# Two transfers of the first batch, a weight slice and a query load, issued later in a hand-ordered attention and gated-MLP kernel on one Trainium2 core

## The chip, the cores and the metric

One core of one Trainium2 chip runs the whole kernel in one launch. The metric is the device time of one execution in microseconds (us), the median over runs. The engines are named as in the profile: PE (matmul), ACT (activations), DVE (VectorE), POOL (GpSimd) and SP (SyncE, which here only issues transfers). Each engine works through its own instructions strictly in order; an instruction that waits holds all that stand behind it.

## The reference

Four batches of eight heads, 768 positions, 64 values per head. Each query and key gets a bucket number from the signs of six random projections; a query attends only to the keys in its bucket. The 3072 x 512 result goes through a gated MLP with a residual.

```python
q_bits = (np.einsum('bhsd,dk->bhsk', q, proj) > 0).astype(np.int64)
k_bits = (np.einsum('bhsd,dk->bhsk', k, proj) > 0).astype(np.int64)
mask = q_bucket[:, :, :, None] == k_bucket[:, :, None, :]
scores = np.where(mask, scale * np.matmul(q, k.transpose(0, 1, 3, 2)), -1000000000.0)
attn = softmax(scores)                  # written out in the reference
x = np.matmul(attn, v)                  # heads side by side: 3072 x 512
gelu = 0.5 * g * (1.0 + erf(g * inv_sqrt2))          # g = x @ w_gate
ffn_out = gelu * (x @ w_val) @ w_out
out = x + 1.0 / (1.0 + np.exp(-(x @ w_res))) * ffn_out
```

## The kernel before

The heads are worked on in pairs: pair p holds two heads, four pairs make a batch, and there are 16 pairs. A pair has nine *chunks* of scores (1024 columns of PSUM each); chunk c belongs to pair c // 9, so that the first batch is chunks 0 to 35 and its fourth pair, p = 3, is chunks 27 to 35. One chunk is some score matmuls (`scores`, L501), one exponential on ACT (L512), and the matmuls with the values (`values`, L476), which the plan places a chunk or more later.

The mask needs no extra pass. The six signs of each query and key are appended to their 64 values as columns of +0.5 and -0.5, one more column holds a constant, and the score matmul contracts over 71 rows, so that a key in another bucket comes out far below. The steps that bring a side of a pair there are, for side 0 (queries) and 1 (keys):

- `load` (L161): the raw values from HBM into `ld`, on SP's queue, 384 KB. `load_v` (L169) does it for the values.
- `tr` (L273) on DVE and `hash` (L284) on PE: the projections, on which the signs depend; `tokens` (L296) brings them back on DVE.
- `cast` (L263 for queries, L265 for keys): the values in bf16 into one of four tiles `nat`.
- `bits` (L305): the signs into `nat`, in four parts of 32 partitions, each on the engine that a letter names: `'vvvp'` is three on DVE and one on POOL.
- then `nat` is transposed into `aug`, either on PE (`turn`, L374, with copies out of PSUM at L382) or by a DMA transpose on SP's queue (`turn_dma`, L361). In the first batch only pair 3 goes by DMA: `('turn_dma', 3, 0)` and `('turn_dma', 3, 1)`.

`vals_a` and `vals_s` (plan names `va` and `vs`, L387 and L395 to L399, on POOL) prepare the values of a pair. `finish` (L420, L421) divides by the sums into `x_tok`; for the first two pairs of the first batch a DMA transpose on SP (L429) follows, from `x_tok` into `x_sb`, for the others PE transposes (`xturn`).

The MLP's weights are bf16 tiles, read from fp32 in HBM by transfers that POOL issues (`load_w`, L248, plan name `w`). There are twelve in a fixed order: first slices of 384 columns, alternately of `w_gate` (`wg`) and `w_val` (`wv`), four each, then `wr`, then three of `wo`. Each `w` in the plan issues the next one. The plan of the first batch has two, so the second is the first slice of `wv`; the other ten are spread over the first gate stage by another list, `BESIDE_GV`. The gate stage (`gv_mm`, L526) follows the 36 chunks; its `wv` matmuls are the first readers of the second transfer.

The order of the first batch is written out by hand, as the list `PLAN` (L17 to L76): it is worked through from first to last, each entry calls the function of its name in `STEP` (L707), and the instructions stand on each engine's queue in the order in which these calls make them. `('S', c)` is the scores and the exponential of chunk c, `('V', c)` its values. Waits between engines follow from the tiles that they share. SP's queue in this stretch is: the loads of the first pairs, the key load of pair 6, the transpose of `x_sb`, the query load of pair 6, the two transposes of pair 3, and then loads of pairs 5 to 7 with a second `x_sb` transpose among them. `ld` has four tiles a side, so a load waits until the pair four back is through.

From the second batch on, a loop with lists of due places takes the part of the plan.

Of the kernel before, what the change touches and what calls it, by code (L numbers as in the profile page):

```python
# [44 lines left out]
    ('S', 12), ('hash', (2, 3), 2), ('hash', (2, 3), 3), ('copy', 1, 1, 6, 12, 'v'), ('cast', 2, 1, 'p'),  # L45
    ('cast', 2, 0, 'p'), ('hash', (2, 3), 0), ('hash', (2, 3), 1), ('finish', 0, 0), ('tokens', (2, 3)),
    ('bits', 2, 0, 'vvp'), ('bits', 2, 1, 'vp'),
# [6 lines left out]
    ('S', 19), ('bits', 3, 0, 'vvvp'), ('turn_dma', 3, 0), ('vs', 2), ('turn', 2, 1, 6, 12, 'f'),  # L54
# [740 lines left out]
```

## Time and profile before

| | |
|---|---|
| time, median of 3 runs | 341.25 us (341.06 to 341.38) |
| the profiled execution: its time, its span | 340.38 us, 338.3 us |
| granted clock of TensorE | 1.0 |
| first batch's chunks | to about 45 us of the span |
| first gate stage | about 45 to 79 us |

The profile is of one execution. Its span is what lies between the first and the last instruction; times in the views are us from the start of the span. "Idle before" is the time for which an engine stood still ahead of an instruction, and its releaser is what ended that. The DMA queue q1 holds what SP issues, q0 what POOL issues. A transfer's time to landing runs from the start of its issue to the arrival of all its data.

### The profile page before, as it was taken

The page shows a single profiled execution, that of the slowest core. Times are in us where ns is not written, and L with a number is a line of the kernel's source. Part 1 is how long each engine was busy: PE and PEld are TensorE (multiplying, and loading weights), DVE is VectorE, ACT ScalarE, POOL GpSimd, SP SyncE. Part 2 cuts the span into 40 slices and gives each one's busy share as a digit, 9 for nine tenths or more (in the row PEclk, how much of TensorE's full clock was granted, in tenths as well). Part 3 has the DMA queues.
Part 4 walks back from the last instruction along what each step waited for, and adds up shares of the span by engine and source line. Part 5 has one row for each costly group of instructions (what it writes and reads, how often), then busy time and mean ns, then how long its engine had stood idle before and what let it go on. Part 6 is the DMA issues. An engine that isn't in the chain of part 4 may idle for free.

```text
span 338.3 us, 7651 instructions
## 1 busy us (share of the span) xinstructions
PE 332.0 (98%) x3042; PEld 201.7 (60%) x3042; DVE 216.3 (64%) x458; ACT 214.1 (63%) x247; POOL 175.3 (52%) x260
## 2 busy tenths in 40 slices
PE   8999899999999999999999999999999999999995
PEld 5767566565666655665666665665566665666443
DVE  8977475554577958876577896877577444433343
ACT  5889962337999952437999981355999984223120
POOL 4788830235299943488799972567889000000000
PEclk9999999999999999999999999999999999999999
DMA  7999999999966223518068933625050360000012
GB/s 240 374 273 166 263 198 150 183 150 238 305 210 145 77 82 84 110 29 186 3 160 236 290 82 93 125 47 94 3 126 33 78 103 31 33 0 2 31 64 93
DMA packets 74387, 43.88 MB, mean 130 GB/s; under 512 B 52544, under 2 KB 71360, under 8 KB 74352
## 3 DMA queue, kind: packets, MB, share of 16 engines
q1 hardware_dynamic: 67872, 37.95, 44.7%
q0 software_dynamic: 6400, 5.44, 10.7%
q8 instruction: 24, 0.39, 0.5%
q14 instruction: 11, 0.09, 0.1%
q10 hardware_dynamic: 80, 0.00, 0.0%
HBM read 29.56 MB, written 6.29 MB: 106 GB/s over the span
## 4 chain that ended last, share of the span: by engine, by line
PE 82%; POOL 9%; DVE 3%; DMA 2%; issue 1%; ACT 1%; SPq 0%; POOLq 0%; DVEq 0%; ACTq 0%
PE sp L526 37%; PE fps L572 14%; PE sp L501 13%; PE av L476 7%; PE rps L558 5%; POOL pr L336 4%; PE hs L284 3%; DMA aug<-nat 2%; POOL v L395 1%; PE wps L229 1%; PE pt L374 1%; DMA x_sb<-x_tok 1%; PE hs L319 1%; DVE sums L342 1%; POOL nat L305 1%
## 5 line engine op out<-in xcount | busy, mean ns | idle before, releaser
L512 ACT ACTIVATE e<-sp 128x1024 bf16<-128x1024 f32 x117 | 117.8, 1027 | 8.6 <-PE sp L501 3.5
L336 POOL TENSOR_TENSOR pr<-ld,projr 128x384 f32<-128x384 f32 x96 | 94.0, 998 | 48.0 <-DVE sums L342 32.2
L543 ACT ACTIVATE gt<-sp 128x768 bf16<-128x768 f32 x48 | 38.9, 811 | 83.7 <-PE sp L526 79.9
L501 PE MATMUL sp<-aug,aug 71*128 71x256 bf16 (+1 forms) x384 | 86.0, 325 | 1.3 <-DMA aug<-nat 0.8
L572 PE MATMUL fps<-wo,hh 128*128 128x512 bf16 (+2 forms) x312 | 79.6, 362 | 0.0
L546 DVE TENSOR_TENSOR hh<-gt,sp 128x768 bf16<-128x768 bf16 x48 | 45.8, 954 | 42.9 <-PE sp L526 39.5
L526 PE MATMUL sp<-x_sb,wg 128*128 128x512 bf16 (+1 forms) x384 | 70.9, 326 | 0.1
L526 PE MATMUL sp<-x_sb,wv 128*128 128x512 bf16 (+1 forms) x384 | 70.9, 326 | 0.0
L476 PEld LDWEIGHTS <-e 128*128 128x128 bf16 x936 | 43.5, 97 | 25.9
L342 DVE TENSOR_REDUCE sums<-pr 128x6 f32<-128x384 f32 x96 | 50.2, 542 | 10.9 <-POOL pr L336 10.5
L526 PEld LDWEIGHTS <-wg 128*128 128x128 bf16 x384 | 37.1, 98 | 25.8 <-issue 1.5
L526 PEld LDWEIGHTS <-wv 128*128 128x128 bf16 x384 | 37.5, 98 | 24.9 <-issue 0.2
L476 PE MATMUL av<-va,e 128*128 128x65 bf16 x936 | 47.0, 193 | 0.0
L572 PEld LDWEIGHTS <-hh 128*128 128x128 bf16 x312 | 28.1, 97 | 21.6
L501 PEld LDWEIGHTS <-aug 71*128 71x128 bf16 x384 | 29.2, 97 | 12.5 <-issue 2.7
L575 DVE SCALAR_TENSOR_TENSOR fps<-th,fps 128x512 f32<-128x512 f32 (+2 forms) x26 | 17.0, 653 | 25.9 <-PE fps L572 25.7
L512 ACT ACTIVATE ering<-sp 128x1024 bf16<-128x1024 f32 x27 | 25.9, 1024 | 2.5 <-PE sp L501 2.3
L558 PE MATMUL rps<-wr,x_sb 128*128 128x512 bf16 x96 | 27.1, 379 | 0.0
L562 ACT ACTIVATE th<-rps 128x512 f32<-128x512 f32 x24 | 14.3, 594 | 18.6 <-PE rps L558 17.5
L273 DVE STREAM_TRANSPOSE t<-ld 128x768 f32<-128x768 f32 (+3 forms) x28 | 23.1, 843 | 0.7 <-PE hs L284 0.6
L455 DVE COPY av<-av 128x390 f32<-128x390 f32 x24 | 13.6, 566 | 14.6 <-PE av L451 14.5
L263 POOL TENSOR_SCALAR nat<-ld 128x768 bf16<-128x768 f32 (+1 forms) x12 | 9.7, 806 | 19.1 <-DMA aug<-nat 17.5
(72 smaller groups left out, 254.6 us busy)
## 6 DMA issues: line engine op xcount, KB each, us to landing
ldv<-in_v_dram SPq DMA_DIRECT2D x16, 384.0 KB, 5.0
out_dram<-o SPq DMA_DIRECT2D x23, 256.0 KB, 2.1
ld<-in_q_dram SPq DMA_DIRECT2D x15, 384.0 KB, 5.1
ld<-in_k_dram SPq DMA_DIRECT2D x15, 384.0 KB, 5.1
wg<-in_moe_w_gate_dram POOLq DMA_DIRECT2D x4, 384.0 KB, 7.4
wv<-in_moe_w_val_dram POOLq DMA_DIRECT2D x4, 384.0 KB, 7.4
wo<-in_moe_w_out_dram POOLq DMA_DIRECT2D x3, 512.0 KB, 7.2
wr<-in_moe_w_res_dram POOLq DMA_DIRECT2D x1, 512.0 KB, 13.7
```

The lines of the kernel that those rows point to most:

```text
L273: nc.vector.transpose(t32[p, side][:, sl].rearrange("p c h n -> p (c h n)"), raw[p, side][:, sl].rearrange("p c d -> p (c d)"))
L336: nc.gpsimd.tensor_mul(pr, raw[x][:, hi * T:(hi + 1) * T], projr[:, bit].unsqueeze(1).to_broadcast([P, T, D]))
L342: nc.vector.reduce_sum(sums[x][:, hi * T:(hi + 1) * T, bit], pr, axis=mybir.AxisListType.X)
L476: nc.tensor.matmul(av[p, hi][:, qt, :], e[:, off:off + P], va[:, hi, jt, 0:D + 1], start=first, stop=(repeats(p, hi) and jt == T - 1), ski ...
L501: nc.tensor.matmul(sp[:, off:off + nq * P], ks[0:KA, hi * T + jt, :], qs[0:KA, hi * T + qt0:hi * T + qt0 + nq, :], start=True, stop=True)
L512: nc.scalar.activation(e, sp, AF.Exp, scale=float(ALPHA))
L526: nc.tensor.matmul(sp[:, c0:c1], w[:, kk, bass.ts(m, P)], xs[:, kk, c0:c1], start=(kk == 0), stop=(kk == KM - 1))
L543: nc.scalar.activation(gt, sp[:, 0:S], AF.Gelu)
L546: nc.vector.tensor_mul(hidden[b][:, m, :], gt, ps[1][:, 0:S])
L558: nc.tensor.matmul(rps, x_sb[b][:, kk, t, :], wr[:, kk, :], start=(kk == 0), stop=(kk == KM - 1))
L572: nc.tensor.matmul(fps[:, cs], hh[:, m, bass.ts(t, P)], wo[:, m, cs], start=(m == 0), stop=(m == KF - 1))
L575: nc.vector.scalar_tensor_tensor(fps[:, cs], th[:, cs], 1.0, fps[:, cs], op0=ALU.add, op1=ALU.mult)
```

## The change

Two entries of `PLAN` move, each to a later chunk. The second `('w',)`, the first slice of `wv`, goes from the head of chunk 13's line to the head of chunk 23's line: on POOL, from between two groups of `bits` to just ahead of `va` of pair 3, past the remaining `bits` of pair 3, a `cast` and the `vs` of pairs 2 and 4. `('load', 6, 0)`, the query load of pair 6, goes from chunk 17's line to chunk 20's: on SP, from ahead of the two DMA transposes of pair 3 to behind them. On POOL and SP nothing else changes its order, and no engine gets another instruction.

```diff
-    ('S', 13), ('w',), ('bits', 3, 1, 'vp'), ('V', 9), ('load', 6, 1),
+    ('S', 13), ('bits', 3, 1, 'vp'), ('V', 9), ('load', 6, 1),
     ('S', 14), ('V', 10), ('turn', 2, 0, 0, 6, 'r'), ('finish', 0, 1),
     ('S', 15), ('turn', 2, 1, 0, 6, 'f'),
     ('S', 16), ('V', 11), ('copy', 2, 1, 0, 6, 'v'),
-    ('S', 17), ('load', 6, 0), ('V', 12), ('V', 13), ('copy', 2, 0, 0, 6, 'v'),
+    ('S', 17), ('V', 12), ('V', 13), ('copy', 2, 0, 0, 6, 'v'),
     ('S', 18), ('cast', 3, 1, 'p'), ('V', 14),
     ('S', 19), ('bits', 3, 0, 'vvvp'), ('turn_dma', 3, 0), ('vs', 2), ('turn', 2, 1, 6, 12, 'f'),
     ('turn', 2, 0, 6, 12, 'r'),
-    ('S', 20), ('turn_dma', 3, 1), ('V', 15), ('copy', 2, 0, 6, 12, 'v'), ('V', 16), ('finish', 1, 0),
-    ('copy', 2, 1, 6, 12, 'v'), ('tr', 4, 1),
+    ('S', 20), ('turn_dma', 3, 1), ('load', 6, 0), ('V', 15), ('copy', 2, 0, 6, 12, 'v'), ('V', 16),
+    ('finish', 1, 0), ('copy', 2, 1, 6, 12, 'v'), ('tr', 4, 1),
     ('S', 21), ('load', 7, 1), ('tr', 4, 0), ('vs', 4), ('load_v', 5), ('V', 17),
     ('S', 22), ('V', 18), ('V', 19),
-    ('S', 23), ('va', 3), ('V', 20), ('cast', 4, 0, 'p'), ('finish', 1, 1), ('cast', 5, 0, 'p'),
+    ('S', 23), ('w',), ('va', 3), ('V', 20), ('cast', 4, 0, 'p'), ('finish', 1, 1), ('cast', 5, 0, 'p'),
     ('tr', 6, 1),
```

## The prediction

> **What bounds the kernel now.** I read the page's busy times first, then the list of waits, then the timelines of PE and ACT around the only wait that concerns the changed lines, then SP, POOL and the DMA queues to see what makes that wait. The page, and two rows of the list of waits over the whole span (engine, line, whom it waited for: us in total, times, longest):
>
> ```profile
> PE 332.0 (98%) x3042; PEld 201.7 (60%) x3042; DVE 216.3 (64%) x458; ACT 214.1 (63%) x247; POOL 175.3 (52%) x260
> PE wps L229 <- PEq L779: 0.8, 1, 0.8
> PE sp L501 <- DMA aug<-nat: 0.8, 1, 0.8
> ```
>
> PE is busy for 98% of the span, so a change can gain little, and only where PE stands still. PE has two listed waits. The first is the start of the program. The second is a score matmul (L501) that waits for a DMA transpose of `nat` into `aug`. The rows of PE and of ACT around it (start us, length us, what, and in brackets the idle time before it and what ended it):
>
> ```profile
> 34.31 0.65 PE L476 MATMUL av<-va,e 128*128 128x65 bf16 x16
> 35.80 0.60 PE L501 MATMUL sp<-aug,aug 71*128 71x512 bf16 x2 [0.84 <-DMA aug<-nat]
> 34.59 1.07 ACT L512 ACTIVATE ering<-sp 128x1024 bf16<-128x1024 f32 x1
> 36.50 7.55 ACT L512 ACTIVATE ering<-sp 128x1024 bf16<-128x1024 f32 x8 [0.84 <-PE sp L501]
> 43.98 1.02 ACT L512 ACTIVATE e<-sp 128x1024 bf16<-128x1024 f32 x1
> ```
>
> The exponentials are one per chunk. The nine of 36.50 to 45.00 are those of the fourth pair (p = 3, chunks 27 to 35), so the row at 35.80 is chunk 27, the first that reads `aug` of pair 3, the pair that the plan turns by DMA (`turn_dma`). PE ended its other work at 34.31 + 0.65 = 34.96 and stood until 35.80. ACT stood 0.84 us as well, and from then to 45.00 it ran without a break. So **0.84 us is lost on both engines at once**, and nothing before or after hides it. Why the transposes came late stands in SP's timeline and one piece of the chain of waits (start, length, what):
>
> ```profile
> 25.04 1.30 SPq L429 DMA_TRANSPOSE x_sb<-x_tok  x1
> 26.40 0.56 SPq L161 DMA_DIRECT2D ld<-in_q_dram  x1
> 27.63 6.19 SPq L361 DMA_TRANSPOSE aug<-nat  x2
> ...
> 30.52 5.23 DMA aug<-nat
> ```
>
> The first transpose of pair 3 was issued at 27.63. The second was issued at 30.52 and landed at 30.52 + 5.23 = 35.75, which is where PE's wait ends. Between them and the transpose of `x_sb` stands the query load that the change moves. The DMA view of 25 to 29 us (queues: packets, MB, share; then issues in the window with us to landing) shows what ran meanwhile; the row after the dots is from the window 32 to 33:
>
> ```profile
> q0 software_dynamic: 469, 0.36, 89.8%
> q1 hardware_dynamic: 26, 0.03, 2.3%
> issues: line engine op xcount, KB each, median us to landing
> wv<-in_moe_w_val_dram POOLq DMA_DIRECT2D x1, 384.0 KB, 5.6
> ld<-in_q_dram SPq DMA_DIRECT2D x1, 384.0 KB, 5.3
> x_sb<-x_tok SPq DMA_TRANSPOSE x1, 5.6
> aug<-nat SPq DMA_TRANSPOSE x1, 6.8
> ...
> q1 hardware_dynamic: 39, 0.01, 161.3%
> ```
>
> q0 carries POOL's transfers and q1 SP's. For four us nearly all that moved was the weight slice, and SP's queue moved 26 packets, although the transpose of `x_sb` had been issued at 25.04 and the load at 26.40. So everything on SP's queue started some 3 us late, the load's 384 KB went ahead of the first `aug` transpose, and the second, behind all of it, hardly moved from 32 to 33.
>
> **The change part by part.** It removes no instruction and adds none; one DMA issue of POOL and one of SP stand elsewhere in their queues, and with them the two transfers. The rows of POOL, and the part of the bits that VectorE writes:
>
> ```profile
> 24.27 0.85 POOL L248 DMA_DIRECT2D wv<-in_moe_w_val_dram  x1
> 25.20 0.98 POOL L305 TENSOR_SCALAR nat<-ht 32x72 bf16<-32x72 f32 x2
> 26.24 0.82 POOL L265 CAST nat<-ld 128x768 bf16<-128x768 f32 x1
> 27.15 0.45 POOL L305 TENSOR_SCALAR nat<-ht 32x72 bf16<-32x72 f32 x1
> ...
> 31.80 0.82 POOL L387 CAST va<-ldv 128x768 bf16<-128x768 f32 x1
> ...
> 34.56 0.83 POOL L263 TENSOR_SCALAR nat<-ld 128x768 bf16<-128x768 f32 x1 [1.10 <-DMA aug<-nat]
> ...
> 25.97 0.68 DVE L305 TENSOR_SCALAR nat<-ht 32x72 bf16<-32x72 f32 x3
> ```
>
> *The weight issue on POOL.* It holds POOL from 24.27 to 25.20, 0.93 us, ahead of the last four POOL pieces that pair 3's transposes need. It is moved past them and past both groups of value sums (L395 to L399), to just ahead of the `va` cast at 31.80. So the last bits, which ended at 27.15 + 0.45 = 27.60, end at 26.67; VectorE's share of them ends at 25.97 + 0.68 = 26.65, and SP is free of `x_sb` at 26.34. The first transpose can then be issued at about 26.70 instead of 27.63. The issue itself comes at 31.80 - 0.93 = 30.87; behind it POOL is where it was.
>
> *The weight transfer.* It leaves the stretch in which it kept SP's queue still. For how transposes go without it there are two nearby places, the four issues after 57.64 and the one `aug` issue of the window 59.2 to 61; the last row is that of the eight L429 transposes, shortest, median and longest:
>
> ```profile
> 57.64 7.00 SPq L361 DMA_TRANSPOSE aug<-nat  x4
> ...
> aug<-nat SPq DMA_TRANSPOSE x1, 4.0
> ...
> DMA to landing us min/median/max: 2.7/3.5/5.6
> ```
>
> Four issues in 7.00 us are 1.75 each, with a landing 4.0 after the issue. From 26.70, that puts the second issue at 28.45 and its landing at 32.5. With the spacing and the landing of the old run (30.52 - 27.63 = 2.89, then 5.23) it would be 26.70 + 2.89 + 5.23 = 34.8. Both are ahead of 34.96. I take 32.5, because weight and load are both away, and keep 34.8 as the slow end. *Sum of this part:* the wait goes, 0.84 us.
>
> *The query load on SP* (`load 6,0`) goes behind both transposes: SP's queue is rid of 384 KB in front of them, and its issue of 0.56 us. It now leaves at 26.70 + 2 x 1.75 = 30.2, at the slow end at 26.70 + 6.19 = 32.9, and with 5.3 to land it is there at 35.5 or 38.2. Who waits for it: VectorE's transpose of `ld`, and behind that on VectorE the two divisions of finished pairs, whose PSUM tile PE wants again at the head change of chunk 31:
>
> ```profile
> 35.95 0.97 DVE L273 STREAM_TRANSPOSE t<-ld 128x768 f32<-128x768 f32 x1
> 37.53 0.20 DVE L420 RECIPROCAL rec<-av 128x6 f32<-128x6 f32 x1 [0.61 <-PE av L448]
> 37.76 0.56 DVE L421 TENSOR_TENSOR x_tok<-av,rec 128x384 bf16<-128x384 f32 x1
> 42.35 0.20 DVE L420 RECIPROCAL rec<-av 128x6 f32<-128x6 f32 x1 [4.03 <-PE av L448]
> 42.15 0.28 PE L476 MATMUL av<-va,ering 128*128 128x65 bf16 x4
> ```
>
> At the slow end the transpose runs from 38.2 to 39.2 and the division (0.20 + 0.56) ends by 40.0; PE wants the tile at 42.15 - 0.84 = 41.3. So the move costs nothing, covered by VectorE's idle 0.61 and 4.03 us; past a landing of 39.5 it would cost one for one. The loads behind it on SP (k and q of pair 7, two of v) lose the same place, but they had been issued behind transposes that kept SP until 33.8, so they are issued earlier or at the same time.
>
> *The weight slice in its new place* is read first by the `wv` matmuls:
>
> ```profile
> 46.94 1.14 PE L526 MATMUL sp<-x_sb,wv 128*128 128x512 bf16 x6
> ```
>
> Issued at 30.87 with 5.6 to land it is there at 36.5, and 15 us are free until 46.94 - 0.84 = 46.1. POOL's wait of 1.10 at 34.56 for the first transpose goes too; POOL is not what PE waits for there, so I count it at nothing.
>
> *What is late next.* With `aug` there, chunk 27 starts when PE is through, at 34.96. ACT could start it at 34.59 + 1.07 = 35.66 and needs PE's first scores 0.70 after their start (36.50 - 35.80), again 35.66. From ACT's steady pace (7.55 less a last one of 1.03, over seven: 0.93) the gap of 36.50 - 34.59 = 1.91 would shrink by 0.98. That is the upper end; PE's 0.84 is the lower, and I take it, since PE is full until 45. After 45 PE works without a break, and whatever is on the chain later starts from PE:
>
> ```profile
> 91.75 0.26 PE av L476 x8
> ...
> 93.36 1.00 POOL pr L336
> ...
> 124.11 2.74 DMA x_sb<-x_tok
> ```
>
> The long POOL stretch that ends in the DMA at 124.11 is begun by values of PE at 91.75, so it moves along with them.
>
> *A rule against the working.* The 469 packets to 26 say that the weight slice kept the transposes off. The Trainium skill, DMA: Bandwidth & Descriptors, section Queues, rings and completion order, says that each DMA engine takes turns between queues, a packet at a time. By it the slice would have cost the transposes a share of the bandwidth and not a standstill; the trace of 25 to 29 does not agree, at least not for transposes that begin. By the rule taking the slice away would bring little beyond POOL's 0.93 us, the landing would be nearer 34.8 than 32.5, and the sum the same 0.84 with 0.14 us to spare; so its place is in the first rival's chance.
>
> **The sum.** The profiled execution took 340.38 us (span 338.3 and 2.08 around it); less 0.84 it is 339.54. The three runs have a median of 341.25, 0.87 above the profiled one, so the forecast is 341.25 - 0.84 = **340.4**, from 340.1 (0.98 gained, and the runs' own 0.16 below) to 340.7.
>
> **The rivals.**
> 1. *The wait is only shortened, or stays.* The row of 32 to 33 speaks for it: the second transpose hardly moved with no weight in flight and the load mostly through, so part of the slowness is the transposes' own. Against it: even with the old spacing and landing, the 0.93 us of POOL alone exceed the 0.84 of the wait. A landing between 34.96 and 35.75 gives 340.4 to 341.25, in the middle 340.8.
> 2. *The weight slice meets the second transpose in its new place: slower.* In the old place `x_sb` took 5.6 to land where the shortest of its kind took 2.7, so the slice cost it 2.9. If the transposes keep the old spacing, the second is in flight until 34.8, and the slice, issued at 30.87, comes into it: 34.8 + 2.9 = 37.7, a wait of 2.7 in place of 0.84, and 343.1. If only the landing is slow (28.45 + 5.23 = 33.7, then + 2.9 = 36.6), the wait is 1.6 and the time 342.0. It decides from a landing past 35.75. Against it: undisturbed, the second transpose has landed at 32.5, about when the slice's first packets can come.
> 3. *The edit does what it says and the time does not follow*: the chain at 124.11 waits for a transfer, and a later transfer that keeps its old time could take the gain back. Then 341.25. The order on POOL and SP itself is fixed by the plan, so that the edit does not move the issues can be left out.
>
> **How the numbers follow.** Forecast 0.70, rival 1 0.15, rival 2 0.10, rival 3 0.05. A measurement of this kernel tells about 0.2%, 0.68 us, from no change, so faster means under 340.57, and the forecast lies only 0.16 inside it, as much as single runs differ. Of the forecast's 0.70 I count 0.59 as faster and 0.11 as same; of rival 1, 0.03 and 0.12; rival 3 is same; rival 2 is slower but for 0.01. Faster 0.62, same 0.29, slower 0.09. The range takes in the forecast, rival 1 and rival 3 with the runs' 0.16 above: 340.1 to 341.4; it leaves out rival 2.
>
> **What would show it.** In the new profile: POOL's four pieces directly one behind another from 24.27; the first `aug` transpose issued near 26.7 and the second landed by 32 to 35; no wait of PE at L501 for `aug`, ACT's exponentials of pair 3 following on those of pair 2 without a gap and ending near 44.2; the `wv` issue near 30.9; VectorE's transpose of the moved load with at most 2.3 us of waiting and no wait of PE behind it; the first `wv` matmul at 46.1 in place of 46.94, and all later stages earlier by the same amount. A wait of PE at chunk 27 that is as long or longer, ended by the second transpose while q0 moves, would prove rival 2; a wait gone with the later stages not earlier, rival 3.

## The result, and the profile after

| | before | changed |
|---|---|---|
| time, median of 22 runs each | 341.04 us (340.51 to 342.74) | 340.11 us (339.14 to 342.25) |
| ratio, 95% interval | | 0.9973 (0.9962 to 0.9984) |
| profiled execution: time, span | 340.38, 338.3 us | 340.49, 338.4 us |

The ratio is 0.92 us less (0.55 to 1.30). The page of the changed kernel, and all that the list of waits has for PE over the whole span:

```profile
span 338.4 us, 7652 instructions
...
PE 333.1 (98%) x3042; PEld 202.8 (60%) x3042; DVE 216.2 (64%) x458; ACT 213.9 (63%) x247; POOL 175.0 (52%) x260
...
PE wps L229 <- PEq L779: 0.8, 1, 0.8
```

PE's wait for `aug` is gone. Yet this span is no shorter than the old one, and the first thing to learn is why. ACT's timeline of the changed kernel (start, length, what, idle before):

```profile
9.03 3.99 ACT L512 ACTIVATE ering<-sp 128x1024 bf16<-128x1024 f32 x4
...
23.62 8.63 ACT L512 ACTIVATE ering<-sp 128x1024 bf16<-128x1024 f32 x9 [0.53 <-PE sp L501]
32.14 3.77 ACT L512 ACTIVATE e<-sp 128x1024 bf16<-128x1024 f32 x4
35.76 8.52 ACT L512 ACTIVATE ering<-sp 128x1024 bf16<-128x1024 f32 x9
44.20 1.02 ACT L512 ACTIVATE e<-sp 128x1024 bf16<-128x1024 f32 x1
```

The same for the kernel before:

```profile
7.86 3.99 ACT L512 ACTIVATE ering<-sp 128x1024 bf16<-128x1024 f32 x4
...
22.45 8.63 ACT L512 ACTIVATE ering<-sp 128x1024 bf16<-128x1024 f32 x9 [0.53 <-PE sp L501]
```

From the first exponential to chunk 13's it is 14.59 us in both. The changed kernel's execution only began 1.17 us later, in a part that the change does not touch. So the stretch to compare is the one that holds the change: **from the start of chunk 13's exponential to the end of chunk 35's**, 45.00 - 22.45 = 22.55 us before and 45.22 - 23.62 = 21.60 in the changed kernel. That is 0.95 less, and ACT runs without a gap. From there to the end it is 293.3 and 293.2 us. SP, POOL, and the landing times of the changed kernel:

```profile
26.21 1.30 SPq L429 DMA_TRANSPOSE x_sb<-x_tok  x1
27.88 3.20 SPq L361 DMA_TRANSPOSE aug<-nat  x2
31.13 0.95 SPq L161 DMA_DIRECT2D ld<-in_q_dram  x1
...
23.86 2.56 POOL L305 TENSOR_SCALAR nat<-ht 32x72 bf16<-32x72 f32 x5 [1.82 <-DVE ht L296]
26.48 0.82 POOL L265 CAST nat<-ld 128x768 bf16<-128x768 f32 x1
27.39 0.45 POOL L305 TENSOR_SCALAR nat<-ht 32x72 bf16<-32x72 f32 x1
...
32.02 0.85 POOL L248 DMA_DIRECT2D wv<-in_moe_w_val_dram  x1
...
x_sb<-x_tok SPq DMA_TRANSPOSE x1, 2.8
...
L361 SPq DMA_TRANSPOSE aug<-nat x2: 1420/1574/1728, 27.9 to 29.4; - x2
...
DMA to landing us min/median/max: 5.2/5.3/5.4
```

Take 1.17 off each to compare with the kernel before. The first transpose goes out at 26.71 (before: 27.63). `x_sb` lands in 2.8 instead of 5.6. The second transpose goes out at 29.4 and lands at about 34.6, which is 33.4 on the clock of the kernel before, where PE is through at 34.96.

In all runs below I give the landing of the second transpose as the time since chunk 13's exponential began: the need is 34.96 - 22.45 = 12.5, the kernel before has 35.75 - 22.45 = 13.3, the changed one 34.6 - 23.62 = 11.0. The 34.96 is the end of PE's last matmuls as the profile models it, so the need is known to 0.2 us or so: in the changed kernel, where nothing is waited for, chunk 27's score matmul begins at 35.96, which is 12.3.

### The profile page after: what moved, and what is told of

Its sections match the earlier page's. It is cut to its first block, busy times and chain, and to the rows that moved or that the text cites. A ratio compares the mean times of both kernels' runs of the same rounds, so it can differ in the third digit from the quotient of the medians.

```text
span 338.4 us, 7652 instructions
## 1 busy us (share of the span) xinstructions
PE 333.1 (98%) x3042; PEld 202.8 (60%) x3042; DVE 216.2 (64%) x458; ACT 213.9 (63%) x247; POOL 175.0 (52%) x260
## 4 chain that ended last, share of the span: by engine, by line
PE 83%; POOL 8%; ACT 4%; DVE 3%; issue 1%; DMA 1%; POOLq 0%; DVEq 0%; ACTq 0%
PE sp L526 37%; PE fps L572 14%; PE sp L501 14%; PE av L476 7%; PE rps L558 5%; POOL pr L336 4%; PE hs L284 3%; ACT ering L512 3%; ACT e L512 1%; PE hs L319 1%; PE wps L229 1%; PE pt L374 1%; POOL v L395 1%; DMA x_sb<-x_tok 1%; DVE sums L342 1%
## 5 line engine op out<-in xcount | busy, mean ns | idle before, releaser
L572 PEld LDWEIGHTS <-hh 128*128 128x128 bf16 x312 | 28.1, 97 | 21.6
L501 PEld LDWEIGHTS <-aug 71*128 71x128 bf16 x384 | 29.3, 97 | 11.5 <-issue 2.7
## 6 DMA issues: line engine op xcount, KB each, us to landing
wr<-in_moe_w_res_dram POOLq DMA_DIRECT2D x1, 512.0 KB, 13.9
```

Of the source, the lines that this page charges most:

```text
L501: nc.tensor.matmul(sp[:, off:off + nq * P], ks[0:KA, hi * T + jt, :], qs[0:KA, hi * T + qt0:hi * T + qt0 + nq, :], start=True, stop=True)
L572: nc.tensor.matmul(fps[:, cs], hh[:, m, bass.ts(t, P)], wo[:, m, cs], start=(m == 0), stop=(m == KF - 1))
```

## The experiments

Ten edits and one repeat; the profile of each, taken of one of its runs, gave the stretch of chunks 13 to 35, PE's wait at chunk 27 as the list of waits has it, and the landing.

| run | median us | ratio to before, 95% | stretch us | PE's wait us | landing |
|---|---|---|---|---|---|
| weight alone | 340.43 | 0.9978 (0.9964 to 0.9992) | 21.71 | none | 12.4 |
| load alone | 340.26 | 0.9975 (0.9959 to 0.9992) | 21.61 | none | 12.4 |
| weight beside | 344.24 | 1.008 (1.0042 to 1.0119) | 27.80 | 1.4 | 13.9 |
| POOL held | 340.63 | 1.0005 (0.9978 to 1.0032) | 21.60 | none | 11.8 |
| POOL held, again | 341.52 | 1.0003 (0.9975 to 1.0031) | 21.60 | none | 11.5 |
| two slices | 349.2 | 1.0214 (1.0184 to 1.0243) | 30.63 | 3.1 | 15.6 |
| weight early | 340.11 | 0.9974 (0.9958 to 0.9991) | 21.60 | none | 11.1 |
| load between | 340.36 | 0.998 (0.9966 to 0.9994) | 21.60 | none | 12.1 |
| weight between sums | 341.13 | 1.0005 (0.9988 to 1.0021) | 22.50 | 0.8 | 13.3 |
| held, no slice | 340.19 | 0.9973 (0.9961 to 0.9985) | 21.61 | none | 11.5 |
| fetch shifted | 341.43 (one run) | | 21.60 | none at chunk 27 | 10.2 |

### Each part alone

```diff
-    ('S', 13), ('w',), ('bits', 3, 1, 'vp'), ...
+    ('S', 13), ('bits', 3, 1, 'vp'), ...
-    ('S', 23), ('va', 3), ...
+    ('S', 23), ('w',), ('va', 3), ...
```

> Only the weight slice is moved; the query load stays ahead of the two transposes. Measured by the stretch from the start of chunk 13's exponential to the end of chunk 35's, 22.55 us in the kernel before and 21.60 in the changed one, and by PE's wait for aug at chunk 27, 0.84 and none. Theory A (the slice in flight keeps SP's queue from moving): x_sb lands about 2.8 after its issue instead of 5.6, and even with the load's 384 KB (some 1.2 us) in front the second transpose lands about 1 us ahead of need: no wait, stretch 21.6. Rival B (only POOL's 0.93 us of issue counts): no wait either, but with x_sb still 5 us in landing. Rival C (the load in front is what makes the transposes late): the wait stays over 0.5 us, stretch over 22.2.

```diff
-    ('S', 17), ('load', 6, 0), ('V', 12), ...
+    ('S', 17), ('V', 12), ...
-    ('S', 20), ('turn_dma', 3, 1), ('V', 15), ...
+    ('S', 20), ('turn_dma', 3, 1), ('load', 6, 0), ('V', 15), ...
```

> Only the query load is moved; the weight slice stays at chunk 13. Theory A: x_sb still lands some 5.6 after its issue and the first transpose is issued late by POOL, but 384 KB less stand in front, which took about 0.9 to 1.2 us: the second transpose lands about 1 us earlier, at or just before the need, wait 0 to 0.2, stretch 21.6 to 21.8. Rival B (only POOL's issue counts): the wait of 0.84 stays, stretch 22.5. Rival C (the load is all of it): no wait and the second transpose landed more than 1 us before PE is through.

Issues and landing, the weight alone and then the load alone:

```profile
L361 SPq DMA_TRANSPOSE aug<-nat x2: 1441/2232/3022, 27.7 to 29.2; - x2
...
DMA to landing us min/median/max: 6.2/6.3/6.3
```

```profile
L361 SPq DMA_TRANSPOSE aug<-nat x2: 2527/2572/2616, 28.8 to 31.5; - x2
...
DMA to landing us min/median/max: 4.5/5.2/5.9
```

With the weight alone the second transpose goes out at 29.2 and lands 6.2 to 6.3 later, near 35.5; chunk 13 began at 23.10, so 12.4. With the load alone it goes out at 31.5 and lands in 4.5, at 36.0; chunk 13 began at 23.63, so 12.4 again. **Either part takes away the listed wait by itself**, but with next to no margin; together they land at 11.0, 2.3 us earlier than before where each alone gives 0.9. Adding the gains of the two parts would have counted one wait twice.

The weight alone leaves a trace of the wait: chunk 27's score matmul begins at 35.61, 12.5 after chunk 13's exponential against 12.3 in the changed kernel, and the stretch is 0.1 longer. I had expected 1 us of margin there. Part of what is missing is in the profile: from 34.50 to 35.25 us the slice, now in its new place, moves 178 packets and SP's queue 34, when the second transpose should end.

`x_sb` tells theory A from rival B: it landed in 2.9 us with the weight alone and in 5.8 with the load alone. Rival B fell with the load alone as well: POOL's issue was where it had been, and the wait was gone. Rival C fell with the weight alone. The weight alone moves POOL's issue and the transfer at once; what POOL's lateness is worth is in the held runs below.

### The slice in other places

```diff
-    ('S', 23), ('w',), ('va', 3), ...
+    ('S', 23), ('va', 3), ...
-    ... ('turn_dma', 3, 0), ('vs', 2), ...
+    ... ('turn_dma', 3, 0), ('w',), ('vs', 2), ...
```

> As the changed kernel, but the weight slice is issued right behind the last bits of pair 3, so that POOL's issue is out of the way and the transfer runs beside the transposes. Theory A: the slice's first packets come while the transposes of pair 3 are due and hold them for its 2 us of data and more; the second transpose lands 35.0 to 36.5 on the clock of the kernel before, wait 0.1 to 1.5, stretch 21.7 to 23. Rival B (POOL's issue is what counts): no wait, stretch 21.6. By the rule of taking turns the transposes would lose a share only, about 1 us, and the wait would stay under 0.3.

The wait is 1.4, at the upper end of theory A, but the profiled execution took 345.9 us, where 341.04 + 1.4 - 0.84 = 341.6 was to be expected. The wait row, and the table of stages (us, PE busy, PEld, DVE, ACT, POOL, granted clock, DMA share, GB/s):

```profile
PE sp L501 <- DMA aug<-nat: 1.4, 1, 1.4
...
36.00:38.00 2.00, 1.14 (x14) 0.76 (x15) 0.61 (x2) 0.60 (x2) 1.92 (x3) 1.00 1.10 370
38.00:40.00 2.00, 1.92 (x21) 0.72 (x20) 1.54 (x3) 2.00 (x3) 1.92 (x6) 0.77 1.12 344
40.00:42.00 2.00, 2.00 (x24) 1.39 (x21) 0.00 (x0) 1.28 (x2) 2.00 (x4) 0.50 1.09 377
...
48.00:50.00 2.00, 2.00 (x27) 1.45 (x29) 0.56 (x1) 1.29 (x2) 0.00 (x0) 0.67 1.31 203
50.00:52.00 2.00, 2.00 (x42) 1.36 (x35) 1.48 (x3) 1.98 (x2) 0.00 (x0) 1.00 1.31 203
```

PE stood from 35.46 to 36.86, and from about 39 to 49 us its granted clock was 0.50. In that time PE, not ACT, was the bound (ACT waited 0.7 us ahead of nearly every chunk). Of the ten runs of this kernel five had a mean clock of 0.983 to 0.985 and took 345.9 to 346.6 us; the other five, at 0.999 to 1.0, took 341.35 to 342.6. The table's 344.24 lies between the two groups, whose medians are 346.3 and 342.2: the half clock goes with 4 us more. How long PE stood in the runs of the second group no profile shows.

```diff
-    ('S', 13), ('w',), ('bits', 3, 1, 'vp'), ...
+    ('S', 13), ('w',), ('w',), ('bits', 3, 1, 'vp'), ...
-    (0, 'w'), (0, 'w'), (3, 'w'), ...
+    (0, 'w'), (3, 'w'), ...
```

> The kernel before with the suspected cost doubled: a second weight slice is issued right behind the first at chunk 13 (and one slice fewer in the gate stage). Theory A (a slice in flight keeps the transposes on SP's queue from starting until its data is through): a second 384 KB, some 2 us of data, holds them 2 us longer, so PE's wait at chunk 27 grows from 0.84 to about 2.8, and as the wait of 1.4 us in the run with the slice beside the transposes was followed by 10 us at a granted clock of 0.50, this one is too: stretch of chunks 13 to 35 26 to 30 us, time 344 to 348. Rival B (POOL's issue alone): POOL is held 0.8 longer, the wait grows to 1.6 to 1.7 and no more. By taking turns: between 1.7 and 2.2.

```profile
PE sp L501 <- DMA aug<-nat: 3.1, 1, 3.1
...
38.00:40.00 2.00, 0.00 (x0) 0.00 (x0) 1.52 (x3) 0.29 (x1) 0.57 (x1) 1.00 1.28 288
40.00:42.00 2.00, 1.31 (x11) 0.76 (x12) 0.00 (x0) 0.17 (x1) 1.84 (x4) 0.55 0.93 214
...
52.00:54.00 2.00, 2.00 (x22) 1.60 (x21) 0.86 (x3) 1.41 (x2) 0.00 (x0) 0.54 1.31 203
```

Twice the slice made 2.3 us more of wait, near theory A's 2.0 and far from the 0.8 of POOL's issue alone. The stretch of 30.6 and the time of 349.2 lie above what I had expected; all four runs had a mean clock of 0.979 to 0.985. And theory A is right only in part: `x_sb` begins to move near 31.5 us, while the second slice goes on until about 36, so that from there on transposes and slice run side by side. The DMA view of this run, 33.0 to 33.5 us (packets, MB, share):

```profile
q0 software_dynamic: 90, 0.07, 89.2%
q1 hardware_dynamic: 90, 0.02, 39.7%
```

From 32.25 to 34.0 us it is 317 packets each, 0.24 MB of the slice and 0.08 of the transposes. Alone, in the changed kernel from 33.25 to 33.75, the transposes move 564 packets in half a us. So **a slice in flight does two things: transposes that have not begun stay away until it is nearly through, and those that have begun move packet for packet with it**, at about a sixth of their pace. With the slice beside, 31.25 to 33.25 us, it was 347 packets to 241.

```diff
-    ('S', 6), ('w',), ('turn', 1, 0, 0, 6, 'r'), ...
+    ('S', 6), ('w',), ('w',), ('turn', 1, 0, 0, 6, 'r'), ...
-    ('S', 23), ('w',), ('va', 3), ...
+    ('S', 23), ('va', 3), ...
```

> As the changed kernel, but the second slice goes out with the first at chunk 6, long before the transposes of pair 3, instead of behind them. Theory A: what counts is only that no slice is in flight from 25 to 35; the wait at chunk 27 stays away, the stretch of chunks 13 to 35 is 21.6, x_sb lands in about 2.8. POOL is held 0.9 us longer at 17, ahead of casts for pair 2 which PE turns at 23.4; if that is late, PE waits there up to 0.9 and the time is that of the kernel before. Otherwise as the changed kernel, 340.1. Rival (the place behind the transposes matters, since the transfers late in the batch profit from it): a new wait between chunk 27 and the gate stage.

No wait, the stretch and the time as in the changed kernel. What counts is that the slice is away from the transposes, not that it comes later. It was not quite away: a few of its packets still went by until about 28.5 us, and `x_sb` landed in 3.8 us, not in the 2.8 that I had expected.

```diff
-    ... ('vs', 4), ('load_v', 5), ...
+    ... ('w',), ('vs', 4), ('load_v', 5), ...
-    ('S', 23), ('w',), ('va', 3), ...
+    ('S', 23), ('va', 3), ...
```

> As the changed kernel, but the weight slice is issued 2.06 us earlier, between the two groups of value sums (about 28.8 on the clock of the kernel before, with its first packets near 30 to 31). Theory A: the second transpose is under way by then and is caught by the slice in part: landing 0 to 2 us later than in the changed kernel (33.5 on the same clock), so between no wait and 0.6; in single runs more, with the clock drop. If the slice waits for SP's queue to be empty, as it did in the changed kernel's run, nothing changes: 340.1 and stretch 21.6.

Two us earlier than in the changed kernel is already too early: the old wait of 0.8 is back, and the time is that of the kernel before. I had expected 0 to 0.6. The slice's packets begin only near 33.75 us, when nearly all of the second transpose has moved, but from 34 to 35 us they are all that moves, 240 packets and none on SP's queue, and the transpose lands at 36.5, 7.5 us after its issue. Why its end waits there, where transposes and slice elsewhere take turns, no run shows.

### The load between the transposes

```diff
-    ... ('turn_dma', 3, 0), ('vs', 2), ...
+    ... ('turn_dma', 3, 0), ('load', 6, 0), ('vs', 2), ...
-    ('S', 20), ('turn_dma', 3, 1), ('load', 6, 0), ...
+    ('S', 20), ('turn_dma', 3, 1), ...
```

> As the changed kernel, but the query load goes between the two transposes of pair 3. Theory A: its 384 KB, 1.2 us of data, come in front of the second transpose only, which lands about 1.2 us later than in the changed kernel, near 34.7 on the clock of the kernel before against a need at 34.96: no wait or up to 0.3, stretch 21.6 to 21.9. Rival D (a change from transpose to plain transfer and back on the queue costs a standstill of its own, some 1.2 us each, as the gaps in the packets suggest): the second transpose lands 2 to 4 us later, wait 0.9 to 2.7, with a clock drop above about 1.4.

The landing is 12.1, 1.1 later than in the changed kernel, as theory A had it from the 384 KB alone; rival D falls.

### POOL held without a transfer

```diff
+    def hold():
+        for _ in range(3):
+            nc.gpsimd.memset(projs, 0.0)
-    ('S', 13), ('bits', 3, 1, 'vp'), ...
+    ('S', 13), ('hold',), ('bits', 3, 1, 'vp'), ...
```

> As the changed kernel, but POOL is held at chunk 13, where the weight issue had been, by three memsets of a tile that is not used any more (projs, about 0.32 us each), without any transfer. Theory A: the first transpose is issued 0.9 us later than in the changed kernel, with its landing times unchanged, so the second lands 0.9 later, still ahead of need: no wait or under 0.2, stretch 21.6 to 21.8. Rival B: the wait of 0.84 comes back, stretch 22.5.

> The held kernel once more, unchanged: five of its twelve runs took 342 to 346 us although their mean granted clock was 0.994 to 1.0, and its profile, of a run without that, shows no wait at chunk 27. If the later transposes meet the slice now and then (theory A: in this kernel the slice too is issued 1 us later, so they should not), the runs over 342 are there again, with a wait of PE at chunk 27 in a profile that catches one. If they came from outside the kernel, the times are 339.6 to 340.8 as in the run that holds POOL with the slice early.

The same hold in the kernel with the slice early:

> As the run with the slice early at chunk 6, and POOL held at chunk 13 by the three memsets of the held run (1.05 us). It tells what POOL's lateness alone does, since no slice can meet the late transposes. Theory A: the second transpose lands about 1 us later than with the slice early and still before the need; no wait, stretch 21.6, 340.1 and none of the runs of 342 to 346 us that made up five of twelve with the slice behind. Rival B (POOL's hold does harm by itself): those runs are there again, or the time is 340.6 to 341.2.

All three profiles say the same: 1.05 us more on POOL, a landing 0.4 to 0.8 later than without the hold, no wait at chunk 27, stretch 21.6. Holding POOL alone does not bring the wait back. The times do not settle so well. With the slice early the ten runs lie between 339.57 and 341.05. With the slice behind, five of twelve runs and then seven of twelve took 341.3 to 345.7, all but one at a mean clock of 0.999 to 1.0, so it was not the half clock; neither profile is of such a run. Where those us went is **open**.

### PE's instruction fetch

```diff
-    ('fill', 6),
+    ('fill', 65, 32),
```

> As the changed kernel, with the six warming matmuls of 512 columns at the start replaced by 65 of 32 columns, which puts 118 more instructions on PE's stream and does not touch anything later. In all profiles so far one packet of the queue of instructions (q8) goes by 31 to 32 us, and about half a us behind it the transposes of pair 3 stand still for 1.0 to 1.3 us. If that packet causes the standstill and is PE's fetch, both move some 2 to 3 us earlier, relative to chunk 13's exponential, and the second transpose lands up to 1.2 us earlier, at 32.3 to 33.5 on the clock of the kernel before. If the standstill is the transposes' own, it stays between the two transposes while the packet moves. The stretch of chunks 13 to 35 stays at 21.6.

First the changed kernel, DMA view from 31.25 to 31.5 us, then from 31.75 to 33; then the shifted one from 27.0 to 27.5, with its issues and landing:

```profile
q8 instruction: 1, 0.02, 22.0%
...
q1 hardware_dynamic: 27, 0.01, 5.3%
```

```profile
q8 instruction: 1, 0.02, 14.6%
...
L361 SPq DMA_TRANSPOSE aug<-nat x2: 1427/1560/1693, 28.9 to 30.4; - x2
...
DMA to landing us min/median/max: 3.7/3.9/4.1
```

In the changed kernel one packet of 0.02 MB goes by on the queue of instructions, and from 31.75 to 33 the transposes' queue moves 27 packets where it otherwise moves about 1000 a us. With 118 more instructions on PE that packet is at 27.0 to 27.5, ahead of both transposes; there is no standstill between them, and they land 3.7 to 4.1 us after their issue instead of 5.2 to 5.4, as expected. The packet moved further than expected, by 4.8 us relative to chunk 13's exponential. **With the packet elsewhere, the standstill between the transposes is gone**, which speaks against its being their own. That the packet causes it is likely and not shown: this is one profile, and in two others the standstill did not come half a us behind the packet but 1.5 us (two slices: 35.0, then 36.5) and 2 us (load between: 31.2, then 33.3). The time of this kernel says nothing: its start is another, and it has a new wait of 0.4 us for a transpose of `x_sb` at a later gate stage.

## Why the prediction was right, and where it was off

- *The wait at chunk 27 is what the change removes*: right, and so is the sign and the size: 340.4 forecast, 340.11 measured, at the low end of the range. Of the 0.29 between them 0.21 is the base, three runs at 341.25 where 22 have 341.04; the gain is 0.92 against 0.84, and in the stretch 0.95, so that ACT's pace (0.98) was the nearer of the two bounds and not PE's row.
- *POOL's 0.93 us and the first issue at 26.70*: 26.71 measured. *The weight issue at 30.87*: 30.85; its landing took 7.8 us and not 5.6, still long before the first `wv` matmul at 47.16. *The load's issue at 30.2*: 29.96. Nothing waits for the load:

```profile
37.12 0.97 DVE L273 STREAM_TRANSPOSE t<-ld 128x768 f32<-128x768 f32 x1
```

- *The second landing at 32.5*: mis-sized, it was 33.4. The step took the landing of 4.0 from a place after 57 us; here it was 5.2, and the 1.2 us between is the standstill of 31.75 to 33, which was gone with PE's instructions shifted. The first rival's reading, that from 32 to 33 the slowness is the transposes' own, was wrong for the same reason, as far as that one profile shows.
- *The slice kept SP's queue still*: right in kind; `x_sb` 2.8 against 5.6, and the doubled slice 2.3 us more of wait. It holds for a transpose that has not begun; one that has begun is slowed. But the sum of its parts had more in it than the wait: weight and load were each worth nearly the whole of it, which the working did not say.
- *The second rival*, the slice meeting the transposes in its new place, did not happen here, with little room: 2 us earlier it does, and with the weight alone its edge shows. Its price was mis-sized. For a wait of 1.6 I gave 342.0; the kernel whose profile has a wait of 1.4 took 341.35 to 342.6 in half of its runs, near what the step gives, and 346 in the other half. The step counted a longer wait as idle time alone, and left out that PE's clock can fall.
- *The rule against the working*: the Trainium skill, DMA: Bandwidth & Descriptors, section Queues, rings and completion order, lets the queues take turns packet by packet. Between plain transfers the trace agrees; the changed kernel, 37.5 to 38.5 us, slice beside loads:

```profile
q0 software_dynamic: 125, 0.10, 60.9%
q1 hardware_dynamic: 116, 0.18, 56.5%
```

Beside transposes that are moving it agrees too, in packets as the profile counts them: 90 to 90 with two slices. What the working had wrong is what the rule would cost: it took a small share, but a packet of the transposes carries a third of the bytes of one of the slice (0.08 MB to 0.24 in 317 packets each), and turn for turn they fall to a sixth of their pace. It does not cover the start: in the kernel before, from 26.5 to 28.75 us, the slice moved 390 packets and SP's queue none, although the transpose of `x_sb` had been issued at 25.04. Nor does it cover the standstill behind the packet of instructions. Why, no run shows.

## What to carry to other kernels

Several causes can stand behind one wait, and each may be enough to remove it: count the wait once, and give each cause its margin in us instead of a share of the gain. Keep DMA transposes that PE waits for clear of transfers on other queues, since here they shared by packets and theirs were the small ones, and look for what a moved transfer meets in its new place, since 2 us decided here. When runs scatter by more than the effect, compare a stretch of the trace that holds the change, between two instructions that both kernels have.

## What was not expected of the hardware

**The clock falls after a short stand of PE.** In the profile of the slice beside the transposes a stand of 1.40 us is followed by some 10 us at 0.50, and five of ten runs of that kernel have a mean clock like the profiled one's; with two slices it is a stand of 3.1 us and all four runs. Of the 75 runs of the kernel before that stood beside all but the repeat, whose profile has a stand of 0.84 us, two have 0.983 (345.88 and 346.06 us). None of the 75 runs of six kernels without the wait (changed, weight alone, load alone, weight early, load between, held with no slice) fell under 0.996. Each kernel's stand is known from one run only, so that how the odds go with its length is not shown. The Trainium skill, TensorE: Matmul & The Clock Gate, section HAM oscillation, warns of gaps of PE over about 3.4 us; here the clock fell behind one of 1.40.

**The start of an execution varies.** Before and changed, the same eight matmuls after the same warming:

```profile
3.89 1.08 PE L319 MATMUL hs<-t,projs 128*128 128x128 f32 x8
```

```profile
3.89 1.94 PE L319 MATMUL hs<-t,projs 128*128 128x128 f32 x8
```

The first exponential began between 7.86 and 10.49 us in the profiles of these kernels. That is most of the scatter between profiles: in the changed kernel and the seven runs with no wait at chunk 27 and the same start of the program (six edits and the repeat), the spans are 337.6 to 338.8 us, and what follows the first exponential is 329.4 to 329.8. The Trainium skill, TensorE: Matmul & The Clock Gate, Part 1, says that the clock's activity window runs free of the kernel's start. Matmuls that take nearly twice as long would fit a clock that rises later; but the view gives a granted clock of 1.00 for both stretches, and no run here tests it.
